# Attention and experts on one core: the spread of the softmax sums moved from GpSimd to VectorE's reciprocal, with four smaller moves around the first pairs

## The chip, the cores and the metric

The kernel runs on one core of a Trainium2 chip. The core's engines are PE (TensorE, matmuls and transposes), DVE (VectorE), ACT (ScalarE) and POOL (GpSimd); SP only issues transfers. Each runs its own instructions in the order in which they stand, and waits for the others through semaphores. The metric is device time of one execution in microseconds, as the median of several runs.

## The reference, cut to what matters

```python
q, k, v: (2, 8, 1152, 64)           # batch, heads, positions, head size
q_pool = q.reshape(B, H, S // 2, 2, D).mean(axis=3)      # 576 pooled rows a head
scores = scale * q_pool @ k.T
scores = scores - scores.max(-1)
attn = exp(scores)
attn = attn / (attn.sum(-1) + 1e-09)
x = attn @ v                         # then to (B * S / 2, H * D) = (1152, 512)
p = domain_probs / (domain_probs.sum(-1) + 1e-09)
for e in range(4):
    out += p[:, e:e + 1] * (relu(x @ w1[e]) @ w2[e])     # 512 -> 1024 -> 512
```

## The kernel before

**Pairs and tiles.** Attention goes over 8 pairs of heads (pair 0 to 7, `n` in the code). A pair has nine tiles of 128 pooled rows by 1152 keys; tiles 0 to 7 belong to one head each, tile 8 holds the last 64 rows of both. Matmuls take fp32 operands split into a high and a low part, so each q and k is split (`pool_split`: POOL writes the high part, then the difference), and k and q halves are moved to the other partitions by transfers within SBUF (`stack_k`, `move_q`).

**The way of a tile.** PE writes its scores to PSUM. DVE reads them once, scales, negates, takes the minimum and writes them to SBUF (`neg_scores`, line 440: called the pass over the scores below). ACT takes exp and sums each row (`exps`). PE transposes the result in blocks of 64, ACT and DVE copy half of the transposed blocks each (`transposed`, lines 336 and 338), and PE multiplies by v (`PV_part`, line 472).

**Rounds.** A pair has five rounds (`round_`, `r` from 0 to 4), each for two tiles, round 3 for one. In a round PE transposes a finished tile, writes scores of a tile three ahead, transposes the seam (the last block of one tile and the first of the next), writes the second scores, transposes the second tile, and does a part of the product with v. PSUM has two sides for scores, which are used in turn, so that new scores wait until DVE's pass has read the old ones of that side.

**Blocks prepared for later pairs.** At the end of a round PE transposes blocks for other purposes into a side of PSUM that is free by then (`prepare`): the next pair's q (`item_q`) and k (`item_k`), and the inverse sums (`item_r`). With `defer` the copy out of PSUM is put off until the next round has transposed its first tile (`waiting`). In round 3 of pairs 1 to 5 the blocks of the next k stand `beside` the seam in the same PSUM region `tp`.

**The sums.** The output of a group of tiles is scaled by 1 / sum. `inv_sums` runs in round 0 (for the pair before, tiles 4 to 8) and in round 2 (tiles 0 to 3): DVE adds 1e-9 and takes the reciprocal of 4 or 5 numbers a row, POOL copies each of the first four over 64 columns into `spread` (line 481), PE transposes `spread` at the end of the round, and DVE copies the result to `rb`.

**Behind a round.** What an output tile needs afterwards (its split, or sums and differences of blocks for the Strassen-like scheme of the experts) is put in `behind` and runs on POOL, in pair 6 with `all_split`: three sums and four splits in a row. POOL also prepares w1 in the last pairs (`w1_sums`, `w1_lo`).

**The start.** SP issues q and k of pair 0, then of pair 1, then v of pair 0 and the stacking of its k (`stack_k0`), held behind a marked instruction by a `nop` on SP (`behind_q`).

```python
pn, grp, k0, k1 = ((n - 1, 1, 0, 5), (n - 1, 1, 5, 9), (n, 0, 0, 3), (n, 0, 3, 6), (n, 0, 6, 9))[r]
```

That line of `round_` says which pair's and group's product with v, and which of the nine key blocks, stand in which round.

Of the kernel before, what the change touches and what calls it, by code (L numbers as in the profile page):

```python
# [17 lines left out]
def attention_moe_kernel(ctx, tc, q, k, v, probs, w1, w2, out):  # L18
    nc = tc.nc
    B, H, S, D = q.shape  # L20
    NT, DM = out.shape
    E, _, FF = w1.shape
    P = 128
# [124 lines left out]
    with ExitStack() as actx:  # L148
# [122 lines left out]

        def join_k(c, dst=None):
            t0, t1 = KTS[c]
            nc.gpsimd.tensor_copy(
                (kc[c] if dst is None else dst).rearrange("p (t h d) -> p t h d", h=2, d=D), kn[:, :, t0:t1].rearrange("p h t d -> p t h d"))

        def split_k(n, c, src):
# [56 lines left out]
        def copy(eng, dst, src):  # L334
            if eng is nc.scalar:
                nc.scalar.activation(dst, src, AF.Copy)  # L336
            else:
                nc.vector.tensor_copy(dst, src)  # L338

        def prepare(items, pt, defer=False):  # L340
            blocks = [b for bl, _ in items for b in bl]
            pt = half_transposes(blocks, pt)

            def used():
                at = 0
                for bl, use in items:
                    use(pt[:, :, at:at + len(bl)])
                    at += len(bl)
            return used if defer else used()

        tiles = []
        for n in range(NP):
# [93 lines left out]
            nc.scalar.activation(sx[g % 3], sx[g % 3], AF.Exp, bias=mn[g % 3], scale=-1.0,  # L446
                                 accum_out=sums[n % 2][:, i:i + 1])

        def transposed(parts, pt, engs):
            pt = half_transposes([sx[g % 3][:, kt * P:(kt + 1) * P] for g, k0, k1 in parts for kt in range(k0, k1)], pt)  # L450
            at = 0
            for g, k0, k1 in parts:
                n, i = tiles[g]
                src = pt[:, :, at:at + k1 - k0]
                at += k1 - k0
                if i == 8:
                    dst = aT[1][:, :, k0:k1, 256:320]
                else:
                    j, h = divmod(i, 2)
                    dst = aT[j // 2][:, h, k0:k1, (j % 2) * P:(j % 2 + 1) * P].rearrange("p k (a x) -> p a k x", a=2)  # L460
                if len(engs) == 1:
                    copy(engs[0], dst, src)
                else:
                    for a in range(2):
                        copy(engs[a], dst[:, a], src[:, a])

        def PV_part(n, grp, k0, k1):
            po = PVB
# [7 lines left out]
        def inv_sums(n, grp):  # L476
            c0, c1 = ((0, 4), (4, 9))[grp]
            r = rs[n % 2][:, c0:c1]
            nc.vector.tensor_scalar_add(r, sums[n % 2][:, c0:c1], 1e-9)
            nc.vector.reciprocal(r, r)  # L480
            nc.gpsimd.tensor_copy(
                spread.rearrange("p (c x) -> p c x", x=HALF), r[:, :4].unsqueeze(2).to_broadcast([P, 4, HALF]))

        def split_x(op, kt, c, src, eng):
            hi, lo = xop(op, 0, kt)[:, c], xop(op, 1, kt)[:, c]
# [97 lines left out]
        neg_scores(1)  # L583
        join_k(0)
        join_k(1)
        join_k(2, xr[:, 1, :4 * P])
        prep_q0()
        summed = add_q(nc.gpsimd)
        behind_q = nc.sync.nop()
        tc.add_manual_dep(behind_q.ins, summed.ins.name, SYNC, reason="loads behind the second q")  # L590
        load_kv(vn[0], v, 0)
        stack_k0()
        scores(2, 1, 0, True)
# [18 lines left out]
        both = (nc.scalar, nc.vector)  # L612
        pending = [2]
        first = [1]
        waiting = []

        def round_(n, r, items=(), spare=(), beside=(), wide=False, before=None, mid=None, defer=False, swap=True):
            ts_ = [g for g in ((9 * n + 5,) if r == 3 else [9 * n + (-1, 1, 3, 0, 6)[r] + j for j in range(2)]) if g >= 0]
            x, count, side = ts_[0], len(ts_), first[0]
            f = x + 3  # L620
            transposed([(x, 0, 8)], tp, both)
            while waiting:
                waiting.pop(0)()
            if before:
                before()
            rest = scores(f, count, side, wide)
            transposed([(x, 8, 9)] + [(g, 0, 1) for g in ts_[1:]], tp, both[:1])
            if beside:
                prepare(beside, tp[:, :, HALF:])
            for g in pending:  # L630
                exps(g)
            pending.clear()
            neg_scores(f)
            if count == 2:
                scores2(f + 1, rest)
                transposed([(ts_[1], 1, 9)], tp, both)
                exps(f)
                neg_scores(f + 1)
            pending.append(f + count - 1)
            if mid:  # L640
                mid()
            pn, grp, k0, k1 = ((n - 1, 1, 0, 5), (n - 1, 1, 5, 9), (n, 0, 0, 3), (n, 0, 3, 6), (n, 0, 6, 9))[r]
            if pn >= 0:
                PV_part(pn, grp, k0, k1)
                if k1 == KT:
                    finish(pn, grp)
            if items:
                used = prepare(items, SIDE[side if count == 2 else 1 - side], defer)
                if defer:
                    waiting.append(used)  # L650
                if count == 2 and swap:
                    first[0] = 1 - side
            if spare:
                prepare(spare, tp)
            while behind:
                behind.pop(0)()

        for n in range(NP):
# [3 lines left out]
            if n == 0:  # L662
                round_(0, 0, [item_k(1, 1, nc.scalar), item_k(1, 2, nc.scalar)], wide=True)
            elif n == 1:
                round_(1, 0, [item_k(2, 1, nc.scalar), item_k(2, 2, nc.scalar)], [item_r(0, 1, nc.vector)],
                       before=lambda: inv_sums(0, 1), defer=True)
            else:
                round_(n, 0, [item_r(n - 1, 1, nc.vector)], before=lambda: inv_sums(n - 1, 1))
            if n and two:
# [10 lines left out]


            if n == 0:
                round_(0, 1, [item_q(1, nc.scalar)], wide=True, mid=lambda: stack_k(1, 0, 4), swap=False)
            elif n == 1:
                round_(1, 1, [item_q(2, nc.scalar)], defer=True)
                stack_k(2, 0, 4)
            else:
                round_(n, 1)
                if not last:
                    move_q(n + 1, 1)  # L690
# [6 lines left out]
            if n == 1:  # L697
                round_(n, 2, r0, before=lambda: inv_sums(n, 0))
                move_q(2, 0)
                stack_k(2, 4, 9)  # L700
                move_q(2, 1)
            else:
                round_(n, 2, r0, before=lambda: inv_sums(n, 0), swap=n > 0)
            if n == 0:
                stack_k(1, 4, 9)
                move_q(1, 1)
# [17 lines left out]


            if n and two:
                round_(n, 3, [item_q(n + 2, nc.scalar)], beside=[item_k(n + 2, 1, nc.scalar)], defer=True)
            else:
                round_(n, 3)
            if n and not last:  # L730
# [8 lines left out]


            if n and two:
                round_(n, 4, [item_k(n + 2, 2, nc.scalar)], defer=True)
                stack_k(n + 2, 0, 4)
            else:
                round_(n, 4)
# [190 lines left out]
```

## Time and profile before

| what | value |
|---|---|
| median of 3 runs | 640.75 us (639.38 to 641.59) |
| the profiled execution | 640.39 us, span 638.6 us |
| PE busy | 610.0 us, 96% of the span |
| DVE, ACT, POOL busy | 362.5, 297.5, 347.5 us |
| attention with its way out | 0 to about 264 us |
| experts | about 264 to 638.6 us |
| mean granted clock of PE | 0.982 |

The times of rows and windows are counted in the profiled execution from the start of its span. Busy time counts an engine's instructions whether or not the next engine waits for them, so what an engine is worth is read from who waits for whom. [...]

### The profile page before, as it was taken

What the parts mean: (1) busy time and instruction counts of PE and PEld (TensorE: products, weight loads), DVE (VectorE), ACT (ScalarE), POOL (GpSimd) and SP (SyncE); (2) the same over time, 40 slices, a digit from 0 to 9 for tenths busy, and PEclk for the clock granted to TensorE, in tenths of its full rate; (3) what the DMA queues carried; (4) which work ended last, traced back from release to release, by engine and by line L of the source; (5) the groups of instructions that cost most, each with busy time, mean ns of one, the idle gap of its engine ahead of it and who ended that gap; (6) DMA issues with size and microseconds to landing.
All of it is one profiled execution on the core that took longest, in us unless ns stands there. A gap on an engine that the chain in (4) does not pass through costs nothing.

```text
span 638.6 us, 12467 instructions
## 1 busy us (share of the span) xinstructions
PE 610.0 (96%) x5045; PEld 515.2 (81%) x5045; DVE 362.5 (57%) x564; ACT 297.5 (47%) x545; POOL 347.5 (54%) x411
## 2 busy tenths in 40 slices
PE   8888899999999688999999999999999999999997
PEld 7656677777777566799899899899889889989986
DVE  6667486787877563954544454454454454454454
ACT  5756567677776553462343243144144135135030
POOL 4626635446460664795674584584484485485140
PEclk9999799999999977999999999999999999999999
DMA  4793684673925100111111111121121121120105
GB/s 149 166 246 102 150 209 126 129 189 98 217 63 154 34 26 9 59 41 53 48 34 51 49 46 55 34 65 35 35 66 34 34 67 33 34 67 1 33 2 148
DMA packets 41497, 50.90 MB, mean 80 GB/s; under 512 B 3296, under 2 KB 27232, under 8 KB 41440
## 3 DMA queue, kind: packets, MB, share of 16 engines
q1 hardware_dynamic: 40560, 48.94, 29.3%
q10 hardware_dynamic: 880, 1.18, 0.5%
q8 instruction: 39, 0.64, 0.4%
q14 instruction: 18, 0.15, 0.1%
HBM read 30.97 MB, written 2.36 MB: 52 GB/s over the span
## 4 chain that ended last, share of the span: by engine, by line
PE 87%; POOL 5%; DMA 2%; ACT 2%; issue 1%; DVE 1%; SPq 0%; POOLq 0%; DVEq 0%
PE banks L892 31%; PE banks L137 27%; PE banks L472 10%; PE banks L207 8%; PE banks L388 8%; PE banks L380 3%; DMA kk<-kk 2%; POOL xb L490 1%; DVE sx L440 1%; POOL q2all L215 1%; POOL xb L487 1%; ACT aT L336 1%; DMA kq<-in_k_dram 0%; POOL kk L118 0%; ACT sx L446 0%
## 5 line engine op out<-in xcount | busy, mean ns | idle before, releaser
L892 PE MATMUL banks<-w2s,hb 128*128 128x512 f32 (+1 forms) x876 | 199.3, 387 | 0.0
L892 PEld LDWEIGHTS banks<-w2s,hb 128*128 128x128 f32 x876 | 162.5, 188 | 32.7
L896 DVE SCALAR_TENSOR_TENSOR acc<-banks,pw,acc 128x512 f32<-128x512 f32 (+1 forms) x137 | 101.7, 743 | 81.4 <-PE banks L892 81.2
L118 POOL TENSOR_TENSOR kk<-kq,kk 128x512 fp32r<-128x512 f32 x64 | 72.6, 1169 | 116.4 <-ACT kk L110 116.4
L440 DVE TENSOR_SCALAR_CACHE_REDUCE sx<-banks 128x1152 f32<-128x1152 f32 x72 | 97.3, 1352 | 32.3 <-PE banks L207 30.6
L336 ACT ACTIVATE aT<-banks 128x512 f32<-128x512 f32 (+1 forms) x144 | 59.6, 437 | 77.8 <-PE banks L207 76.3
L446 ACT ACTIVATE sx<-sx,mn 128x1152 f32<-128x1152 f32 x72 | 90.7, 1259 | 0.5 <-DVE sx L440 0.5
L812 POOL TENSOR_TENSOR hb<-xr,hb 128x576 fp32r<-128x576 f32 x48 | 68.9, 1444 | 21.0 <-ACT hb L811 21.0
L472 PE MATMUL banks<-aT,vn 128*64 128x320 f32 (+1 forms) x576 | 80.2, 419 | 0.0
L859 ACT ACTIVATE xr<-banks 128x576 f32<-128x576 f32 x14 | 9.1, 653 | 147.7 <-PE banks L137 147.7
L137 PE MATMUL banks<-xb,kk 128*128 128x288 f32 x480 | 76.9, 296 | 0.4 <-ACT xr L819 0.4
L137 PE MATMUL banks<-q2all,kk 128*128 128x288 f32 x448 | 75.1, 296 | 0.0
L388 PE MATMUL banks<-kk,q2all 64*128 64x512 f32 (+1 forms) x504 | 67.9, 385 | 3.2 <-DMA kk<-kk 2.4
L137 PEld LDWEIGHTS banks<-xb,kk 128*128 128x128 f32 x480 | 68.3, 189 | 1.1 <-ACT xr L819 0.6
L207 PEld LDWEIGHTS banks<-ident,sx 64*128 64x128 f32 x1296 | 56.1, 143 | 15.2 <-ACT aT L336 6.9
L207 PE MATMUL banks<-ident,sx 64*128 64x64 f32 x1296 | 66.6, 231 | 1.3 <-DVE rb L338 0.7
L338 DVE COPY aT<-banks 128x512 f32<-128x512 f32 x72 | 49.6, 689 | 26.8 <-PE banks L207 25.8
L137 PEld LDWEIGHTS banks<-q2all,kk 128*128 128x128 f32 x448 | 64.5, 188 | 0.0
L808 DVE TENSOR_TENSOR xr<-banks,xr 128x576 f32<-128x576 f32 x48 | 36.4, 758 | 40.0 <-PE banks L137 39.8
L472 PEld LDWEIGHTS banks<-aT,vn 128*64 128x64 f32 x576 | 38.3, 139 | 24.5 <-issue 1.2
L388 PEld LDWEIGHTS banks<-kk,q2all 64*128 64x128 f32 x504 | 52.3, 195 | 6.5 <-issue 3.1
L137 PE MATMUL banks<-xa,kk 128*128 128x288 f32 x384 | 56.7, 296 | 0.0
(105 smaller groups left out, 627.6 us busy)
## 6 DMA issues: line engine op xcount, KB each, us to landing
kq<-in_moe_w_dram SPq DMA_DIRECT2D x64, 128.0 KB, 2.4
qsf<-in_moe_w_dram SPq DMA_DIRECT2D x16, 512.0 KB, 3.5
q2all<-q2all SPq DMA_DIRECT2D x28, 256.0 KB, 7.5
vn<-in_v_dram SPq DMA_DIRECT2D x8, 576.0 KB, 5.1
kk<-kk SPq DMA_DIRECT2D x14, 320.0 KB, 8.6
kq<-in_k_dram SPq DMA_DIRECT2D x7, 576.0 KB, 6.2
kq<-in_q_dram SPq DMA_DIRECT2D x7, 576.0 KB, 4.1
kk<-kk SPq DMA_DIRECT2D x14, 256.0 KB, 3.8
```

The source lines that it names most:

```text
L118: nc.gpsimd.tensor_tensor(flat(w1s[u % 2][:, 1, a:b]), flat(wf[:, a:b]), flat(w1s[u % 2][:, 0, a:b].bitcast(F32)), ALU.subtract)
L137: nc.tensor.matmul(chain[:, c, :CW], w1s[u % 2][:, a, WI[wo], kt, :], xop(xo, z, kt)[:, c * CW:(c + 1) * CW], start=(first and kt == 0 and ...
L207: nc.tensor.transpose(pt[:, a, j, :], src[r], ident[r, r])
L336: nc.scalar.activation(dst, src, AF.Copy)
L338: nc.vector.tensor_copy(dst, src)
L388: return nc.tensor.matmul(dst, q2[n % 2][ROWS[a], zq, h, t * P:(t + 1) * P], src[n % 2][ROWS[a], zk, cs], start=(j == 0), stop=(j == 2), s ...
L440: nc.vector.tensor_scalar(sx[g % 3].rearrange("p (c x) -> p c x", c=c), view, -INV, None, ALU.mult, ALU.min, accum_out=mn[g % 3])
L446: nc.scalar.activation(sx[g % 3], sx[g % 3], AF.Exp, bias=mn[g % 3], scale=-1.0, accum_out=sums[n % 2][:, i:i + 1])
L472: nc.tensor.matmul(po[h * HALF:(h + 1) * HALF, :w], vn[n % 2][:, h, kt, :], aT[grp][:, h, kt, :], start=(kt == 0), stop=(kt == KT - 1))
L812: nc.gpsimd.tensor_tensor(lo, c, hi.bitcast(F32), ALU.subtract)
L892: nc.tensor.matmul(pc, h[:, a, sl, ts_], w[:, b, sl, c0:c1], start=(m == 0), stop=(m == len(ops) - 1))
L896: nc.vector.scalar_tensor_tensor(ac, pc, pw[:, tt, e:e + 1], ac, ALU.mult, ALU.add)
```

## The change

`inv_sums` writes DVE's reciprocal straight to `spread`, 64 columns for each of the four numbers; a second reciprocal makes the ninth tile's inverse in place. POOL's copy is gone. `defer` and `waiting` are gone: prepared blocks are copied out of PSUM as soon as they are transposed. `beside` blocks are transposed in one go with the seam, and both are read after. In pair 0 the sum of the second q moves from POOL to DVE, its copy from ACT to DVE and ahead of the second pass over the scores (`ahead`), and in round 2 of pair 0 both halves of the first tile's copy go to ACT (`heads`). SP's `nop` waits for the join of the second k instead of the sum of q. In pair 1 the inverse sums are transposed ahead of the next k's blocks.

```diff
         def join_k(c, dst=None):
...
-            nc.gpsimd.tensor_copy(
+            return nc.gpsimd.tensor_copy(
...
-        def prepare(items, pt, defer=False):
-            blocks = [b for bl, _ in items for b in bl]
-            pt = half_transposes(blocks, pt)
-
-            def used():
-                at = 0
-                for bl, use in items:
-                    use(pt[:, :, at:at + len(bl)])
-                    at += len(bl)
-            return used if defer else used()
+        def blocks_of(items):
+            return [b for bl, _ in items for b in bl]
+
+        def use_items(items, pt, at=0):
+            for bl, use in items:
+                use(pt[:, :, at:at + len(bl)])
+                at += len(bl)
+
+        def prepare(items, pt):
+            use_items(items, half_transposes(blocks_of(items), pt))
...
-        def transposed(parts, pt, engs):
-            pt = half_transposes([sx[g % 3][:, kt * P:(kt + 1) * P] for g, k0, k1 in parts for kt in range(k0, k1)], pt)
+        def transposed(parts, pt, engs, beside=()):
+            blocks = [sx[g % 3][:, kt * P:(kt + 1) * P] for g, k0, k1 in parts for kt in range(k0, k1)]
+            pt = half_transposes(blocks + blocks_of(beside), pt)
...
+            use_items(beside, pt, at)
...
             nc.vector.tensor_scalar_add(r, sums[n % 2][:, c0:c1], 1e-9)
-            nc.vector.reciprocal(r, r)
-            nc.gpsimd.tensor_copy(
+            nc.vector.reciprocal(
                 spread.rearrange("p (c x) -> p c x", x=HALF), r[:, :4].unsqueeze(2).to_broadcast([P, 4, HALF]))
+            if grp:
+                nc.vector.reciprocal(r[:, 4:], r[:, 4:])
...
-        join_k(2, xr[:, 1, :4 * P])
+        joined = join_k(2, xr[:, 1, :4 * P])
+        behind_k = nc.sync.nop()
+        tc.add_manual_dep(behind_k.ins, joined.ins.name, SYNC, reason="loads behind the second k")
         prep_q0()
-        summed = add_q(nc.gpsimd)
-        behind_q = nc.sync.nop()
-        tc.add_manual_dep(behind_q.ins, summed.ins.name, SYNC, reason="loads behind the second q")
         load_kv(vn[0], v, 0)
         stack_k0()
...
-            transposed([(x, 0, 8)], tp, both)
-            while waiting:
-                waiting.pop(0)()
+            transposed([(x, 0, 8)], tp, heads)
...
-            transposed([(x, 8, 9)] + [(g, 0, 1) for g in ts_[1:]], tp, both[:1])
-            if beside:
-                prepare(beside, tp[:, :, HALF:])
+            transposed([(x, 8, 9)] + [(g, 0, 1) for g in ts_[1:]], tp, both[:1], beside)
...
+            def prepared():
+                if spare:
+                    prepare(spare, tp)
+                if items:
+                    prepare(items, SIDE[side if count == 2 else 1 - side])
...
                 exps(f)
+                if ahead:
+                    prepared()
                 neg_scores(f + 1)
...
-            if items:
-                used = prepare(items, SIDE[side if count == 2 else 1 - side], defer)
-                if defer:
-                    waiting.append(used)
-                if count == 2 and swap:
-                    first[0] = 1 - side
-            if spare:
-                prepare(spare, tp)
+            if not ahead:
+                prepared()
+            if items and count == 2 and swap:
+                first[0] = 1 - side
...
-                round_(0, 1, [item_q(1, nc.scalar)], wide=True, mid=lambda: stack_k(1, 0, 4), swap=False)
+                round_(0, 1, [item_q(1, nc.vector)], wide=True, before=lambda: add_q(nc.vector), mid=lambda: stack_k(1, 0, 4),
+                       ahead=True, swap=False)
...
-                round_(n, 2, r0, before=lambda: inv_sums(n, 0), swap=n > 0)
+                round_(n, 2, r0, before=lambda: inv_sums(n, 0), heads=both if n else both[:1] * 2, swap=n > 0)
...
-                round_(n, 3, [item_q(n + 2, nc.scalar)], beside=[item_k(n + 2, 1, nc.scalar)], defer=True)
+                round_(n, 3, [item_q(n + 2, nc.scalar)], beside=[item_k(n + 2, 1, nc.scalar)])
```

The other calls of `round_` with `defer=True` lose that argument. Three places show how the instructions stand.

On DVE, in round 2 of a pair (`rs` are the sums of four tiles, `sx` the pass over the scores, `aT` the copy of half a transposed tile, `rb` the spread inverse), it stood before:

```order
L338 COPY aT_89<-banks 128x8x64
L479 TENSOR_SCALAR rs_100<-sums_98 128x4
L480 RECIPROCAL rs_100<-rs_100 128x4
L440 TENSOR_SCALAR sx_86,mn_95<-banks 128x1152
L338 COPY aT_90<-banks 128x8x64
L440 TENSOR_SCALAR sx_87,mn_96<-banks 128x1152
L338 COPY rb_91<-banks 128x2x2x64
```

and with the change:

```order
L338 COPY aT_89<-banks 128x8x64
L481 TENSOR_SCALAR rs_100<-sums_98 128x4
L482 RECIPROCAL spread<-rs_100 128x256
L440 TENSOR_SCALAR sx_86,mn_95<-banks 128x1152
L338 COPY aT_90<-banks 128x8x64
L440 TENSOR_SCALAR sx_87,mn_96<-banks 128x1152
L338 COPY rb_91<-banks 128x2x2x64
```

The order is the same; the reciprocal writes 256 columns instead of 4.

On POOL, where pair 6 passes into pair 7 (`xb` and `q2all` are operands of the experts that are split there, `kq` holds w1), it stood before:

```order
L487 TENSOR_SCALAR xb<-xr 128x256
L490 TENSOR_TENSOR xb<-xr,xb 128x256
L97 TENSOR_TENSOR kq<-kq 128x256 x4
L481 COPY spread<-rs_100 128x256
L487 TENSOR_SCALAR q2all<-xr 128x576
L490 TENSOR_TENSOR q2all<-xr,q2all 128x576
L118 TENSOR_TENSOR kk_74<-kq,kk_74 128x512
```

and with the change:

```order
L490 TENSOR_SCALAR xb<-xr 128x256
L493 TENSOR_TENSOR xb<-xr,xb 128x256
L97 TENSOR_TENSOR kq<-kq 128x256 x4
L490 TENSOR_SCALAR q2all<-xr 128x576
L493 TENSOR_TENSOR q2all<-xr,q2all 128x576
L118 TENSOR_TENSOR kk_74<-kq,kk_74 128x512
```

The copy that stood behind the splits and the sums of w1 is gone there, as in fifteen other places.

On SP, in pair 0 (`vn` is v, `kk_74` the stacking of the first k, `kk_75` that of the second, `q2all` the q of pair 1), the difference is:

```order
 L174 DMA vn_84<-in_v_dram 128x2x576
 L265 DMA kk_74<-kk_74 64x1152 x4
+L293 DMA q2all<-q2all 64x4x256 x2
 L285 DMA kk_75<-kk_75 64x2x512 x2
-L293 DMA q2all<-q2all 64x4x256 x2
 L285 DMA kk_75<-kk_75 64x2x640 x2
```

The move of the second q now stands ahead of the first part of the second k; v and the first stacking stay in front of both, behind another instruction of POOL.

## Rows read from the trace of the kernel before

**Rows 1.** The waits of PE in total; columns: us, times, longest us
```profile
PE banks L207 <- POOL spread L481: 11.7, 3, 5.6
```

**Rows 2.** Timeline of PE, pair 7: start us, us, what, [idle before <-releaser]
```profile
223.52 0.48 PE L207 MATMUL banks<-ident,spread 64*128 64x64 f32 x4 [5.03 <-POOL spread L481]
...
242.28 0.47 PE L207 MATMUL banks<-ident,spread 64*128 64x64 f32 x4 [5.56 <-POOL spread L481]
```

**Rows 3.** Windows: us, busy PE, PEld, DVE, ACT, POOL; PEclk, DMA share, GB/s
```profile
223.52:231.94 8.42, 8.42 (x76) 6.57 (x77) 4.80 (x9) 4.63 (x9) 3.23 (x3) 0.62 0.01 2
137.77:143.59 5.82, 5.82 (x79) 4.23 (x78) 4.75 (x9) 4.00 (x8) 0.00 (x0) 1.00 1.08 223
242.28:248.58 6.30, 6.30 (x43) 4.74 (x44) 2.33 (x3) 1.91 (x3) 4.67 (x6) 0.63 0.07 21
203.26:207.57 4.31, 4.31 (x45) 3.15 (x43) 2.87 (x5) 2.72 (x5) 0.00 (x0) 1.00 0.53 167
66.72:74.90 8.18, 8.18 (x87) 6.14 (x87) 1.88 (x2) 4.28 (x8) 4.05 (x5) 0.62 0.58 147
124.23:129.93 5.70, 5.65 (x86) 4.49 (x86) 3.10 (x5) 4.51 (x8) 3.77 (x5) 1.00 0.15 34
36.68:42.00 5.32, 5.32 (x72) 4.29 (x73) 3.76 (x7) 3.74 (x8) 0.05 (x1) 1.00 1.07 289
126.50:129.93 3.43, 3.38 (x60) 2.96 (x56) 2.06 (x3) 2.80 (x7) 2.22 (x3) 1.00 0.23 51
143.59:146.84 3.25, 3.25 (x57) 2.89 (x55) 2.93 (x5) 1.74 (x4) 2.10 (x4) 1.00 0.91 172
```

**Rows 4.** Groups of DVE by shape: count, busy us, mean ns, idle before
```profile
L480 DVE RECIPROCAL rs<-rs 128x4 f32<-128x4 f32 x8 | 1.4, 178 | 0.3
...
L480 DVE RECIPROCAL rs<-rs 128x5 f32<-128x5 f32 x8 | 1.5, 191 | 0.3
...
L606 DVE RECIPROCAL prs<-prs 128x18 f32<-128x18 f32 x1 | 0.3, 268 | 0.0
...
L338 DVE COPY rb<-banks 128x256 f32<-128x256 f32 x16 | 6.8, 422 | 19.6 <-PE banks L207 19.6
```

**Rows 5.** Timeline of DVE, round 2 of pair 4 and of pair 6
```profile
145.76 0.18 DVE L480 RECIPROCAL rs<-rs 128x4 f32<-128x4 f32 x1
145.85 1.33 DVE L440 TENSOR_SCALAR_CACHE_REDUCE sx<-banks 128x1152 f32<-128x1152 f32 x1
...
147.71 1.35 DVE L440 TENSOR_SCALAR_CACHE_REDUCE sx<-banks 128x1152 f32<-128x1152 f32 x1
...
200.63 1.36 DVE L440 TENSOR_SCALAR_CACHE_REDUCE sx<-banks 128x1152 f32<-128x1152 f32 x1 [0.26 <-PE banks L207]
```

**Rows 6.** Timeline of PE, rounds 0 and 3 of pair 4
```profile
134.92 2.91 PE L472 MATMUL banks<-aT,vn 128*64 128x320 f32 x20
...
149.12 1.94 PE L380 MATMUL banks<-kk,q2all 128*128 128x512 f32 x9
...
151.75 0.46 PE L207 MATMUL banks<-ident,qsf 64*128 64x64 f32 x8 [0.49 <-ACT aT L336]
```

**Rows 7.** Timelines of POOL, SP's queue and PE, pairs 0 and 1
```profile
13.48 0.62 POOL L274 COPY xr<-kq 128x512 f32<-128x512 f32 x1
...
18.79 0.38 SPq L174 DMA_DIRECT2D vn<-in_v_dram  x1
...
36.68 1.27 PE L388 MATMUL banks<-kk,q2all 64*128 64x512 f32 x10 [2.42 <-DMA kk<-kk]
```

**Rows 8.** Timelines of DVE and PE behind the last pair
```profile
262.33 0.49 DVE L499 TENSOR_TENSOR xr<-banks,rb 128x320 f32<-128x320 f32 x1
...
264.23 1.07 PE L137 MATMUL banks<-xb,kk 128*128 128x288 f32 x6 [0.37 <-ACT xr L819]
```

**Rows 9.** Timeline of PE, pair 1
```profile
61.37 0.34 PE L207 MATMUL banks<-ident,spread 64*128 64x64 f32 x4 [1.12 <-POOL spread L481]
...
66.72 0.69 PE L207 MATMUL banks<-ident,qsf 64*128 64x64 f32 x8 [2.44 <-POOL qsf L274]
```

More of the change, by code (lines that the diff above doesn't have):

```diff
@@ L614, in attention_moe_kernel, with round_ @@
         first = [1]
-        waiting = []
-        def round_(n, r, items=(), spare=(), beside=(), wide=False, before=None, mid=None, defer=False, swap=True):
+        def round_(n, r, items=(), spare=(), beside=(), wide=False, before=None, mid=None, ahead=False, heads=both, swap=True):
             ts_ = [g for g in ((9 * n + 5,) if r == 3 else [9 * n + (-1, 1, 3, 0, 6)[r] + j for j in range(2)]) if g >= 0]
@@ L665, in attention_moe_kernel @@
                 round_(1, 0, [item_k(2, 1, nc.scalar), item_k(2, 2, nc.scalar)], [item_r(0, 1, nc.vector)],
-                       before=lambda: inv_sums(0, 1), defer=True)
+                       before=lambda: inv_sums(0, 1))
             else:
@@ L682, in attention_moe_kernel @@
             if n == 0:
-                round_(0, 1, [item_q(1, nc.scalar)], wide=True, mid=lambda: stack_k(1, 0, 4), swap=False)
+                round_(0, 1, [item_q(1, nc.vector)], wide=True, before=lambda: add_q(nc.vector), mid=lambda: stack_k(1, 0, 4),
+                       ahead=True, swap=False)
             elif n == 1:
-                round_(1, 1, [item_q(2, nc.scalar)], defer=True)
+                round_(1, 1, [item_q(2, nc.scalar)])
                 stack_k(2, 0, 4)
@@ L741, in attention_moe_kernel @@
             if n and two:
-                round_(n, 4, [item_k(n + 2, 2, nc.scalar)], defer=True)
+                round_(n, 4, [item_k(n + 2, 2, nc.scalar)])
                 stack_k(n + 2, 0, 4)
```

## The prediction, made before the changed kernel was run

> **What bounds the kernel now.** I read the waits of PE first, since PE does 96% of the span, then the PE timeline at each long wait, then the windows around it for the granted clock, and last the timelines of the engines that PE waits for. PE waits 11.7 us in three places for line 481, POOL's spread copy [rows 1]. Two of them lie in the last pair and take 5.03 and 5.56 us [rows 2]: the copy itself is short, but it is queued on POOL behind the differences and splits of pair 6, and PE has to have it before round 0 and round 2 of pair 7 can end. The third, 1.12 us, is in pair 1 [rows 9].
>
> Behind such a wait PE goes on at a lower clock. [...] So the two waits cost 2.60 and 1.99 us more than they show. From 264.2 on PE streams the experts' products [rows 3, 8]; nothing there is touched.
>
> Between these ends, in pairs 2 to 5, PE hardly waits, but DVE is close behind it. In round 2 of pair 4 DVE's second pass over the scores (line 440) runs from 147.71 to 149.06, and PE's next scores, which overwrite those banks, start at 149.12 [rows 5, 6]. The slack of DVE against PE at that place is 0.06 us. That is the number to remember, since the change puts work on DVE just ahead of it.
>
> **What the change costs and gives.** The sums are made against the profiled execution, 640.39 us (span 638.6); the median of the three runs is 640.75, so 0.36 is added at the end.
>
> *The reciprocal.* It wrote 4 or 5 elements a row and now writes 256. No row shows 256. Its rows are 178 ns for 4 elements, 191 for 5 and 268 for 18 [rows 4]: from 4 to 18 each element costs 90/14 = 6.4 ns. Carried on, 256 elements take 0.268 + 238 x 0.0064 = 1.80 us, which is 1.62 more than now. Below, the nearest row with 256 elements is the copy of line 338 at 0.42 us [rows 4]. Above, the step from 4 to 5 is 13 ns, and 0.268 + 238 x 0.013 = 3.36 us. I take 1.80: it is the slope over 14 elements, the 13 ns one over a single element, and the 0.42 is another operation. [...]
>
> *Round 2 of each pair.* Behind the reciprocal on DVE's queue stand the pass over the scores that PE has finished, the copy of half a transposed tile, and the second pass. PE waits for each of these: the spread's transposes need the first pass to have read their banks, the next tile's transposes need the copy, the next scores the second pass. All three start 1.62 later, so PE's scores of 149.12 start 1.62 - 0.06 = 1.56 later, in pairs 2 to 5: 4 x 1.56 = 6.2. In pairs 6 and 7 DVE waits 0.26 for PE ahead of the first pass [rows 5], which absorbs that much: 2 x 1.30 = 2.6. DVE doesn't carry the delay on, because it waits for PE in the round after.
>
> *Round 0.* The same reciprocal and one for the ninth tile stand there, but PE covers them with 20 products of line 472 (2.91 us [rows 6]) where round 2 has 12. I take 0.1 for each of six pairs, 0.6; the low end is 0, and every further 0.1 us of the instruction would show in full.
>
> *Pair 1.* The 1.12 us for the spread go [rows 9], but DVE's second pass is late by about as much as PE gains; and the gate weights' sums behind it on DVE are waited for by POOL, which joins the k that PE wants at 66.72. I take a loss of 0.6, half of that wait; a gain of 1.7 if the reciprocal is short. The 2.44 us wait at 66.72 stays, and its slow clock too.
>
> *Behind pair 7* DVE is the chain: it ends with line 499 at 262.33, and PE's stream starts at 264.23 [rows 8]. Ahead of it stands the last spread reciprocal with the small one: 1.62 + 0.18 = 1.8.
>
> *The spread copies on POOL.* Removing them removes the two waits of rows 2, 10.6 us, and the low clock behind them, 4.6. What is next there is POOL's own work for pair 7's operands and w1; it no longer stands in front of PE, and it runs through without the gaps in which it waited for PE. At worst it takes back the clock's 4.6.
>
> *v and the first stacking.* SP sent v at 18.79, held until POOL had added q [rows 7]. Now it waits only for the third join, which ends at 14.10 [rows 7]: up to 4.7 us earlier. These five transfers (1.7 MB by their shapes) stood in front of those that PE waits for at 36.68, for 2.42 us [rows 7]. SP's queue now has the q move ahead of the second k's first half; it still waits for a POOL split, so the last stack can't leave 4.7 earlier. I take the wait itself, 2.4; the low end is 0. The add of q goes to DVE where DVE waited for PE, so it is hidden; without that cover its 640 columns would cost 640/256 x 0.42 = 1.05 us, an estimate by the copy of [rows 4].
>
> *Copies at once, the blocks beside the seam.* In round 3 PE waited 0.49 us for ACT to read the seam before it transposed the next k's blocks [rows 6]; now both are transposed in one go and ACT reads after. Four pairs (2 to 5): 2.0. In round 4 ACT's copy of q held PE's second scores: from the tile's transposes to the products with v that round took 3.43 us, round 2 3.25 [rows 3]. That is 0.18 in four pairs, 0.7. ACT's other copies then start a little later, into time in which it waited for PE.
>
> *Sum.* Gains 10.6 + 4.6 + 2.4 + 2.0 + 0.7 = 20.3; losses 6.2 + 2.6 + 0.6 + 0.6 + 1.8 = 11.8; net 8.5 faster. 640.39 - 8.5 = 631.9, on the median's scale 632.3 us.
>
> **Rivals.** *A, the reciprocal is cheap:* at 0.42 us the extra is 0.24, round 2 loses 4 x 0.18 = 0.7, the end 0.4, pair 1 gains 1.7. Gains 22.0, losses 1.1: 619.9. For it speaks only that other operations of DVE run at that rate; against it the 268 ns for 18 elements.
>
> *B, the reciprocal is dearer, and DVE becomes the bound:* beyond 1.80 us every added microsecond counts in rounds 0 and 2 of six pairs, in pair 1 and at the end, about 14 times. It decides from 1.80 + 8.5/14 = 2.4 us, 9.0 ns an element; there nothing is gained, and beyond it the kernel is slower. At the 13 ns step it is 3.36 us, and 632.3 + 14 x 1.56 = 654.1. For it: the 13 ns step from 4 to 5. Against it: the 77 ns from 5 to 18, 5.9 each. [...]
>
> *C, the new waits in round 2 lower the clock* as the wait of 2.44 us at 66.72 did: the stretch behind it took 8.18 us at 0.62, its like in pair 3 took 5.70 at 1.00 [rows 3], 2.48 more. In six pairs that is 14.9, and 647.2. It decides if four pairs are hit (9.9). Against it: after the wait of 2.42 us at 36.68 the clock stayed at 1.00 [rows 3], and the new waits are 1.56 in all, in three pieces with work between.
>
> *D, the first stacking brings nothing,* because the transfers are late by the q move: 634.7, within the likeliest one's range.
>
> **How the numbers follow.** The likeliest case with D: 0.58, its own range 628 to 636. A dearer reciprocal that still gains (7.5 to 9 ns, 635 to 640): 0.16. A: 0.13. B beyond 9 ns: 0.07. C: 0.06. The range 620.5 to 639.5 leaves out B, C and about half of A. No change, for three or five rounds of this kernel, is about 0.3%, here 638.8 to 642.7. Faster by more: 0.58, A's 0.13 and most of the 0.16, 0.83. Slower: B beyond 642.7 and C, 0.11. Within: 0.06.
>
> **What would show it.** The reciprocal's group: 16 of 128x256 with a mean near 1.8 us. PE's waits without POOL's spread, with waits for DVE instead, about 1.6 us in round 2 of each pair, and the distance from one pair to the next up from 27.5 (124.23 to 151.75 [rows 3, 6]) to about 28.4. PE's clock at 9 tenths between 215 and 250. PE's first rows of pair 1 at about 34.3. No wait for ACT ahead of the k blocks in round 3. I am wrong if the reciprocal's mean lies under 1 or over 2.4 us, if the clock drops inside the pairs, or if POOL holds PE in the last pair at another instruction.

## The result, and the profile after

| | before | after |
|---|---|---|
| median | 641.17 us (4 runs, 639.38 to 642.38) | 634.59 us (4 runs, 633.87 to 635.43) |
| ratio | 1 | 0.990, 95% interval 0.9873 to 0.9928 |
| profiled execution; span | 640.39; 638.6 us | 635.43; 633.6 us |
| mean granted clock of PE, a share of full speed | 0.982 | 0.991 |

The change makes the kernel 6.6 us faster by the medians, 5.0 by the two profiled spans; 8.5 was forecast. What follows is read from the profiled executions, so it adds up to 5.0. In the changed kernel the spread reciprocal is line 482, the product with v 474, the output tile's scaling 502, SP's relay 398.

PE's waits in total, the longest groups (us, times, longest us):

```profile
PE banks L380 <- DVE sx L440: 3.9, 7, 0.6
PE banks L207 <- ACT aT L336: 2.9, 6, 0.6
PE banks L207 <- POOL qsf L274: 2.7, 1, 2.7
PE banks L388 <- SPq L398: 2.3, 1, 2.3
PE banks L474 <- DVE xr L502: 1.8, 1, 1.8
PE banks L207 <- DVE sx L440: 1.7, 4, 0.4
PE banks L207 <- DVE aT L338: 1.3, 7, 0.2
```

POOL's spread [rows 1] is gone from the list. New are many short waits for DVE, one of 1.8 us for DVE behind pair 7, and one of 2.3 us for SP. The reciprocal's groups on DVE (count, busy us, mean ns):

```profile
L482 DVE RECIPROCAL spread<-rs 128x256 f32<-128x256 f32 x16 | 28.0, 1753 | 0.6
...
L485 DVE RECIPROCAL rs<-rs 128x1 f32<-128x1 f32 x8 | 0.8, 104 | 0.0
```

PE's timeline in pair 7, where [rows 2] stood, and behind it:

```profile
236.70 0.34 PE L207 MATMUL banks<-ident,spread 64*128 64x64 f32 x4 [0.45 <-DVE sx L440]
...
251.12 3.45 PE L474 MATMUL banks<-aT,vn 128*64 128x320 f32 x24 [1.80 <-DVE xr L502]
```

Windows there (us, busy time of PE, PEld, DVE, ACT, POOL, then PEclk, DMA share, GB/s):

```profile
225.48:231.40 5.92, 5.92 (x78) 4.35 (x76) 5.37 (x11) 4.76 (x12) 5.67 (x9) 1.00 0.00 0
...
236.70:243.00 6.30, 5.53 (x61) 4.11 (x62) 4.17 (x8) 4.32 (x9) 6.05 (x9) 1.00 0.00 0
```

No wait of 5 us is left, and the clock is 1.00 where it was 0.62 and 0.63 [rows 3].

Where the time went is read from the starts of equal instructions in the two traces. In the kernel before:

```profile
40.85 0.71 PE L207 MATMUL banks<-ident,sx 64*128 64x64 f32 x16
...
204.04 1.95 PE L380 MATMUL banks<-kk,q2all 128*128 128x512 f32 x9
...
265.14 1.75 PE L137 MATMUL banks<-q2all,kk 128*128 128x288 f32 x12
```

In the changed kernel:

```profile
67.42 0.69 PE L207 MATMUL banks<-ident,qsf 64*128 64x64 f32 x8 [2.66 <-POOL qsf L274]
...
211.11 1.94 PE L380 MATMUL banks<-kk,q2all 128*128 128x512 f32 x9 [0.56 <-DVE sx L440]
...
260.13 1.75 PE L137 MATMUL banks<-q2all,kk 128*128 128x288 f32 x12
```

The transposes at 66.72 of [rows 9] start at 67.42: **0.70 lost** in the start and pair 1 (forecast: 1.8 gained). Split at the transposes of 40.85, which now start at 42.29 (shown below under the start), that is 1.44 lost in the start, where 2.4 gained were forecast, and 0.74 gained in pair 1, where 0.6 lost were forecast. From there to the end of pair 6 another **6.4 are lost**: the scores of round 3 of pair 6 move from 204.04 to 211.11, which is 7.07 in all (forecast: 5.3 for that stretch, 6.2 + 2.6/2 + 0.5 of round 0 less 2.0 and 0.7). Pair 7 and what follows **gain 12.1**: the experts' products that stood at 265.14 start at 260.13, 5.01 earlier (forecast: 12.0 for that stretch, 10.6 + 4.6 less 1.3, 0.1 and 1.8). So the misses lie at the start and inside the pairs. That the end is right to 0.1 is in part luck. Round 2 of pair 7 costs 1.6 and not 1.3: from the products with v at 234.74 to the scores at 238.58 it is 3.84 us, and in pair 6 of the kernel before it was 2.23. Against that the wait of 0.37 for ACT of [rows 8], for which the forecast had no term, is gone.

**Round 2 of pair 4**, on DVE and then on PE:

```profile
148.57 0.74 DVE L481 TENSOR_SCALAR rs<-sums 128x4 f32<-128x4 f32 x1
149.34 1.75 DVE L482 RECIPROCAL spread<-rs 128x256 f32<-128x256 f32 x1
```

```profile
150.42 1.52 PE L474 MATMUL banks<-aT,vn 128*64 128x256 f32 x12
...
152.37 0.34 PE L207 MATMUL banks<-ident,spread 64*128 64x64 f32 x4 [0.43 <-DVE sx L440]
...
152.97 0.71 PE L207 MATMUL banks<-ident,sx 64*128 64x64 f32 x15 [0.20 <-DVE aT L338]
154.24 1.94 PE L380 MATMUL banks<-kk,q2all 128*128 128x512 f32 x9 [0.56 <-DVE sx L440]
```

The delay reaches PE in three waits of 0.43, 0.20 and 0.56, which add up to 1.19; the rest shows as no wait, only in the starts. From the products with v to these scores it is 3.82 us (150.42 to 154.24), where it was 2.28 (146.84 to 149.12, [rows 3, 6]): 1.54 more, 1.56 was forecast.

**Round 4 of pair 3**, on ACT and on PE:

```profile
130.57 0.81 ACT L336 ACTIVATE raw<-banks 128x768 f32<-128x768 f32 x1 [0.86 <-POOL kk L215]
131.27 0.59 ACT L336 ACTIVATE aT<-banks 128x512 f32<-128x512 f32 x1
```

```profile
131.92 0.34 PE L207 MATMUL banks<-ident,sx 64*128 64x64 f32 x4 [0.59 <-ACT aT L336]
```

This was not forecast. ACT's copy of q, now made at once, writes `raw`, from which POOL still splits the next k; it waits 0.86 us for that, and ACT's half of the transposed tile, which PE needs, stands behind it. From the tile's transposes at 129.46 to the products with v at 133.45 it is 3.99 us, where [rows 3] had 3.43.

**The start**, on PE and on SP's queue:

```profile
37.51 0.32 PE L388 MATMUL banks<-kk,q2all 64*128 64x128 f32 x1 [2.33 <-SPq L398]
...
39.53 2.83 PE L474 MATMUL banks<-aT,vn 128*64 128x256 f32 x12
42.29 0.82 PE L207 MATMUL banks<-ident,sx 64*128 64x64 f32 x16
```

```profile
33.15 1.26 SPq L170 DMA_DIRECT2D kq<-in_q_dram  x1
34.45 0.95 SPq L174 DMA_DIRECT2D kq<-in_k_dram  x1
35.45 0.47 SPq L174 DMA_DIRECT2D vn<-in_v_dram  x1
35.96 1.44 SPq L601 DMA_DIRECT2D pr<-in_moe_domain_probs_dram  x2
```

PE no longer waits for the stacked k. It waits, almost as long, for a `nop` on SP: the relay of `S_rows`. This `nop` waits for one matmul of PE, and a later matmul waits for the `nop`; the reason given in the code is "row tiles of one bank". The relay stands on SP's queue behind four loads and can't run until the last is issued at 37.40. Behind this wait the granted clock is 0.67 on average from 37.51 to 42.29, and 12 products with v take 2.83 us, where they took 1.52 before; before, the 2.42 us wait of [rows 7] lay over the relay, and the clock stayed at 1.00 [rows 3].

### The profile page after: what moved, and what is told of

Its sections match the earlier page's. It is cut to its first block, busy times and chain, and to the rows that moved or that the text cites. A ratio compares the mean times of both kernels' runs of the same rounds, so it can differ in the third digit from the quotient of the medians.

```text
span 633.6 us, 12423 instructions
## 1 busy us (share of the span) xinstructions
PE 608.9 (96%) x5045; PEld 512.6 (81%) x5045; DVE 386.9 (61%) x575; ACT 296.9 (47%) x545; POOL 339.1 (54%) x392
## 4 chain that ended last, share of the span: by engine, by line
PE 84%; DVE 9%; ACT 2%; POOL 2%; issue 2%; SPq 1%; DMA 1%; POOLq 0%; DVEq 0%
PE banks L895 31%; PE banks L137 28%; PE banks L474 9%; PE banks L207 7%; PE banks L388 6%; DVE sx L440 4%; PE banks L380 3%; DVE spread L482 2%; DVE aT L338 2%; POOL kk L215 1%; ACT aT L336 1%; DVE rs L481 1%; ACT raw L336 1%; DMA kq<-in_k_dram 1%; POOL kk L214 0%
## 5 line engine op out<-in xcount | busy, mean ns | idle before, releaser
L336 ACT ACTIVATE aT<-banks 128x128 f32<-128x128 f32 (+1 forms) x145 | 60.0, 437 | 60.3 <-PE banks L207 60.0
L207 PE MATMUL banks<-ident,sx 64*128 64x64 f32 x1296 | 68.6, 229 | 4.5 <-ACT aT L336 2.9
L388 PE MATMUL banks<-kk,q2all 64*128 64x512 f32 (+1 forms) x504 | 66.4, 376 | 2.3 <-SPq L398 2.3
```

The source lines that it names most:

```text
L207: nc.tensor.transpose(pt[:, a, j, :], src[r], ident[r, r])
L388: return nc.tensor.matmul(dst, q2[n % 2][ROWS[a], zq, h, t * P:(t + 1) * P], src[n % 2][ROWS[a], zk, cs], start=(j == 0), stop=(j == 2), s ...
```

## The experiments

My theory after the result: the gain is the two waits of pair 7 with their low clock; the losses are the reciprocal's 1.75 us in round 2, the copy of q made at once in round 4, and the relay on SP, which takes the place of the transfer. The rival: the moves around the reciprocal carry the gain, and the spread by itself gives back what it takes.

**One part alone: the spread.** The kernel before with the new `inv_sums`.

```diff
-            nc.vector.reciprocal(r, r)
-            nc.gpsimd.tensor_copy(
+            nc.vector.reciprocal(
                 spread.rearrange("p (c x) -> p c x", x=HALF), r[:, :4].unsqueeze(2).to_broadcast([P, 4, HALF]))
+            if grp:
+                nc.vector.reciprocal(r[:, 4:], r[:, 4:])
```

> The kernel before with one part of the change alone: the spread by DVE's reciprocal, everything else as it was. My theory: this part carries the gain. It ends the two waits of PE for POOL's spread in the last pair and the low clock behind them (12.1 us in the stretch from pair 7 on, as the changed kernel's trace showed), gives back some 0.7 in pair 1, and costs 1.54 in round 2 of pairs 2 to 5 and 1.05 in pair 6 (7.2): net -5.6, so about 635.6 us against 641.2 of before, and round 4 of pairs 2 to 5 stays at 3.43 us from the tile's transposes to the products with v. Rival: the moves around it (first stacking, copies at once, beside the seam) carry the gain and the long reciprocal takes back what it gives: 639 to 642.

Measured: 637.25 us, ratio 0.9945 (0.9923 to 0.9966), so 3.5 us faster (2.2 to 4.9); the profiled span is 633.0, 5.6 shorter. PE's scores of round 3, in pairs 3, 4 and 5:

```profile
124.86 1.94 PE L380 MATMUL banks<-kk,q2all 128*128 128x512 f32 x9 [0.56 <-DVE sx L440]
...
153.93 1.94 PE L380 MATMUL banks<-kk,q2all 128*128 128x512 f32 x9 [0.56 <-DVE sx L440]
...
182.44 1.94 PE L380 MATMUL banks<-kk,q2all 128*128 128x512 f32 x9 [0.56 <-DVE sx L440]
```

Scores of round 3 start at 95.81, 124.86 and 153.93 in pairs 2 to 4, 29.06 apart, where it was 27.52: the reciprocal costs 1.54 a pair there, and 28.51 - 27.46 = 1.05 in pair 5. By the medians the part alone makes somewhat more than half of the 6.6 us; the time lies between the 635.6 of my theory and the rival's 639 to 642. Its 11 runs lie between 635.0 and 641.3, with the clock between 0.985 and 0.993. In the profiled one (635.15) 12 products with v take 1.77 us at 29.95, with no wait ahead of them, and 1.52 at 34.59. Why time is lost there, and clock in the others, isn't shown.

**The other parts alone.** The changed kernel with DVE's small reciprocal and POOL's copy (the diff above, reversed).

> The changed kernel with the spread as it was before: a small reciprocal on DVE and POOL's copy over 64 columns. My theory: the waits of about 5 us in pair 7 come back with their low clock (+12.1), pair 1 loses 0.7, round 2 of pairs 2 to 6 gets back 7.2: about 634.6 + 5.6 = 640.2 us, no faster than before. Rival: the other moves carry the gain: 634 to 636.

Measured: 639.55 us, ratio 0.9974 (0.9958 to 0.9989), 1.7 faster than before. PE's waits:

```profile
PE banks L207 <- POOL spread L483: 12.4, 3, 5.5
```

The two waits are back (5.04 and 5.55), and all the moves together are worth 1.7 us. So the spread carries the gain: next to these moves it is worth 5.0 us (639.55 to 634.59). Its pairs are 27.37 us apart, so the moves gain 0.15 a pair, not the 0.49 + 0.18 that I had put down.

**The reciprocal made short.** DVE takes the small reciprocal and copies it over 64 columns itself.

```diff
-            nc.vector.reciprocal(
+            nc.vector.reciprocal(r, r)
+            nc.vector.tensor_copy(
                 spread.rearrange("p (c x) -> p c x", x=HALF), r[:, :4].unsqueeze(2).to_broadcast([P, 4, HALF]))
-            if grp:
-                nc.vector.reciprocal(r[:, 4:], r[:, 4:])
```

> The changed kernel, but DVE takes the reciprocal of the 4 or 5 numbers and then copies them over 64 columns itself: 0.18 or 0.19 us and about 0.42 instead of 1.75. My theory: in round 2 the delay of DVE shows nearly in full, so 1.15 us come back in round 2 of pairs 2 to 7 and in the chain behind pair 7, some 0.5 more in pair 1: 7 x 1.15 + 0.5 = 8.5, about 626 us. Rival 1: the second pass over the scores is late for another reason, and the length of the reciprocal is hidden: 634 to 635. Rival 2: only the part over DVE's slack counts and the copy of a broadcast column is as slow as the reciprocal (1.7 us): no change, 634.6, and the copy's rows show it.

Measured: 629.53 us, ratio 0.9833 (0.9807 to 0.9858), 5.1 us below the changed kernel by the medians and 4.3 by the ratios, where 8.5 was expected. The copy takes longer than expected. DVE, in round 2 of pair 4 and of pair 5:

```profile
146.12 0.75 DVE L481 TENSOR_SCALAR rs<-sums 128x4 f32<-128x4 f32 x1
146.90 0.18 DVE L482 RECIPROCAL rs<-rs 128x4 f32<-128x4 f32 x1
147.12 1.12 DVE L483 COPY spread<-rs 128x256 f32<-128x256 f32 x1
...
175.11 0.42 DVE L483 COPY spread<-rs 128x256 f32<-128x256 f32 x1
```

POOL in round 2 of pair 4:

```profile
145.97 0.88 POOL L215 TENSOR_TENSOR xa<-xr,xa 128x320 fp32r<-128x320 f32 x1
146.79 1.30 POOL L185 TENSOR_TENSOR qsf<-kq 128x512 f32<-128x512 f32 x1
```

The same copy takes between 0.29 and 1.26 us (mean 0.87 over 16). In pair 4 it ends at 148.24, 0.15 behind POOL's sum of q, which ends at 148.09. The addition of four numbers ends at 146.87, with POOL's instruction that ends at 146.85. So two of DVE's three instructions seem to wait for POOL, not ahead of their start, as for a semaphore, but within their own duration; the next run tests it. The pairs from 2 to 4 are 28.55 apart, the next two 27.31.

**The same without POOL's influence.** The copy is written as a sum over one element. By my theory it takes 0.3 to 0.45 us in all 16 places, whether POOL runs or not, and the time is about 626 us.

```diff
-            nc.vector.tensor_copy(
-                spread.rearrange("p (c x) -> p c x", x=HALF), r[:, :4].unsqueeze(2).to_broadcast([P, 4, HALF]))
+            nc.vector.tensor_reduce(
+                spread.rearrange("p (c x) -> p c x", x=HALF),
+                r[:, :4].unsqueeze(2).to_broadcast([P, 4, HALF]).unsqueeze(3), AX.X, ALU.add)
```

> [...] As a copy it took 0.29 us where POOL was idle and 1.12 to 1.26 us where POOL ran, 0.87 on average, and ended when POOL's instruction ended. [...] Rival: reading one number 64 times is what is slow (then the sum takes 0.9 us on average too), or DVE's second pass is late for another reason: 629.5.

Measured: 626.07 us, ratio 0.9762 (0.9741 to 0.9782). The group on DVE, and its round 2 of pair 4:

```profile
L483 DVE TENSOR_REDUCE spread<-rs 128x256 f32<-128x256 f32 x16 | 6.7, 420 | 0.5
```

```profile
143.84 0.74 DVE L481 TENSOR_SCALAR rs<-sums 128x4 f32<-128x4 f32 x1
...
144.83 0.42 DVE L483 TENSOR_REDUCE spread<-rs 128x256 f32<-128x256 f32 x1
```

Every one takes 0.42 us, this one too, while POOL runs the same sum of q (144.52, 1.29 us). The rival, that reading a number 64 times is slow, falls. The addition ahead of it still takes 0.74. The pairs are 27.83 apart, where 27.7 was expected.

**The addition left out as well.** The kernel leaves out the 1e-9 that the reference adds to the sums.

```diff
-            nc.vector.tensor_scalar_add(r, sums[n % 2][:, c0:c1], 1e-9)
-            nc.vector.reciprocal(r, r)
+            nc.vector.reciprocal(r, sums[n % 2][:, c0:c1])
```

> As the run with the sum over one element, and the addition of 1e-9 is left out (a sum of exponentials relative to the largest is at least 1, and 1e-9 is lost beside it in fp32). That addition of 4 numbers took 0.20 us where POOL was idle and 0.75 where it ran. My theory: DVE's share in round 2 then falls under the slack, the pairs are 27.4 us apart as they are with POOL's spread, and the time is 0.3 us per pair below the run with the addition: 624 to 625 us. Rival: the pairs are bound by PE already without this, and nothing is gained: as the run with the addition.

Measured: 623.74 us, ratio 0.9721 (0.9704 to 0.9738). PE's scores of round 3 in pair 4:

```profile
146.52 1.94 PE L380 MATMUL banks<-kk,q2all 128*128 128x512 f32 x9
```

They start without a wait, 27.31 behind those of pair 3 (119.21). In pairs 2 to 5 round 2 is PE's again; in pair 6 PE still waits 0.30 there for DVE's second pass.

**The copy of q put off again.** As before the change, for `item_q` in round 3 alone.

```diff
+        def prepare_late(items, pt):
+            pt = half_transposes(blocks_of(items), pt)
+            waiting.append(lambda: use_items(items, pt))
...
             transposed([(x, 0, 8)], tp, heads)
+            while waiting:
+                waiting.pop(0)()
...
-                    prepare(items, SIDE[side if count == 2 else 1 - side])
+                    (prepare_late if late else prepare)(items, SIDE[side if count == 2 else 1 - side])
```

> The changed kernel, but ACT's copy of q out of PSUM in round 3 of pairs 1 to 5 is put off again until round 4 has transposed its first tile. My theory: copied at once it stands ahead of ACT's half of that tile's copy, and waits for POOL, which still reads the buffer for the k's split; PE waits 0.59 us behind it. Put off, round 4 goes from 3.99 back to 3.43 us in pairs 2 to 5: -2.2, about 632.4 us, and PE's wait for ACT's aT in round 4 is gone. Rival: ACT is late there because of the exp ahead of it, and putting the copy off brings nothing: 634.6.

Measured: 632.86 us, ratio 0.9878 (0.9854 to 0.9903). PE's transposes beside the seam in pairs 3 and 4:

```profile
125.21 0.41 PE L207 MATMUL banks<-ident,qsf 64*128 64x64 f32 x8
```

```profile
153.80 0.41 PE L207 MATMUL banks<-ident,qsf 64*128 64x64 f32 x8
```

28.59 apart, against 28.98 in the changed kernel (127.25 to 156.23): 0.4 a pair, where 0.56 was expected; PE's waits for `aT` fall from 2.9 us in 6 places to 0.5 in 2. The span is 3.1 shorter; by the medians it is 1.4 to 1.7, of the intervals' size. Against the spread alone (29.06 apart) these pairs gain 0.47: that is the seam, forecast at 0.49, with round 4's copy of k still made at once.

**The relay set free.** The second v and the probabilities are loaded behind round 4 of pair 0.

```diff
                 load_kv(kn, k, 2)
-                load_kv(vn[1], v, 1)
-                load_probs()
...
                 round_(n, 4)
+            if n == 0:
+                load_kv(vn[1], v, 1)
+                load_probs()
```

> The changed kernel, but the loads of the second v and of the gate's probabilities go out behind round 4 of pair 0 instead of ahead of round 3. In the changed kernel PE waits 2.33 us at 37.51 for a relay on SP's queue that stands behind those loads (SP issues them until 37.40). My theory: SP is free from 35.45 on, PE waits about 0.3 instead of 2.33, the clock does not drop behind it (12 products with v 2.83 us, 1.52 at full clock): 2.0 + 1.3 at the start, of which pair 1 may swallow up to all in its wait for POOL at 67.42 (that wait follows DVE, which follows PE, so I expect most to stay): 631.5 to 633. Rival 1: pair 1's wait swallows it: 634.6 with an earlier PE at 42 and the same at 67.42. Rival 2: PE waits for something else at 37.5, such as the stacked k: no change there at all.

Measured: 631.40 us, ratio 0.9849 (0.9825 to 0.9873), 3.2 below the changed kernel. PE:

```profile
35.93 0.32 PE L388 MATMUL banks<-kk,q2all 64*128 64x128 f32 x1 [0.34 <-SPq L398]
...
37.81 1.52 PE L474 MATMUL banks<-aT,vn 128*64 128x256 f32 x12
39.26 0.71 PE L207 MATMUL banks<-ident,sx 64*128 64x64 f32 x16
```

The wait is 0.34 instead of 2.33, the products take 1.52 instead of 2.83, and the transposes at 42.29 start at 39.26. Pair 1 doesn't swallow it: 67.42 becomes 64.56. Both rivals fall.

**The earlier stacking undone.** `behind_q` and POOL's sum of q come back.

```diff
-        joined = join_k(2, xr[:, 1, :4 * P])
-        behind_k = nc.sync.nop()
-        tc.add_manual_dep(behind_k.ins, joined.ins.name, SYNC, reason="loads behind the second k")
+        join_k(2, xr[:, 1, :4 * P])
         prep_q0()
+        summed = add_q(nc.gpsimd)
+        behind_q = nc.sync.nop()
+        tc.add_manual_dep(behind_q.ins, summed.ins.name, SYNC, reason="loads behind the second q")
```

> The changed kernel, but v and the first k's stacking are held until the second q is summed on POOL, as before the change (the q sum goes back from DVE to POOL for that). My theory: sending them earlier brought nothing, since PE waits for the relay on SP's queue in place of the transfer: within 1 us of 634.6, and if anything faster, since before the change the clock stayed at 1.00 behind that wait (633.5 to 634.6). Rival: the earlier stacking does bring the 2.4 us that I forecast, and another part of the start lost them: about 637.

Measured: 635.46 us, ratio 0.9912 (0.9893 to 0.9931), 0.9 above the changed kernel, within the intervals. I was right on the size and wrong on the sign: PE waits longer for the transfer,

```profile
37.17 2.29 PE L388 MATMUL banks<-kk,q2all 64*128 64x512 f32 x11 [3.47 <-DMA kk<-kk]
```

and is at 43.82 where the changed kernel is at 42.29, of which 0.4 is left at the end of the span. The earlier stacking does its work; the relay hides it.

**The gate weights behind the joins**, in pair 1.

```diff
-            if n == 1:
-                gate_weights()
             if n and two:
                 add_q(nc.gpsimd)
                 join_k(0)
                 join_k(1)
+            if n == 1:
+                gate_weights()
```

> The changed kernel, but in pair 1 POOL's products for the gate weights stand behind the sum of q and the joins of the next k instead of ahead of them. In the changed kernel PE waits 2.66 us at 67.42 for the last of those joins, at which the gate weights, which wait for DVE's sums until 63.63, hold POOL for 2.5 us. My theory: the joins then start when their transfer and the split ahead of them allow, PE's wait goes, and with it the low clock behind it (products with v 2.83 us instead of 1.52, the stretch 67.42 to 76 at 0.66): -2.7 to -5, so 630 to 632 us. Rival: the joins wait for the transfer of q and k or for the pieces of kq, and it stays at 634.6.

Measured: 632.21 us, ratio 0.9868 (0.9844 to 0.9891). The wait of 2.66 us at 67.42 (2.44 before, [rows 9]) is gone:

```profile
64.47 0.46 PE L207 MATMUL banks<-ident,qsf 64*128 64x64 f32 x8
64.87 1.52 PE L474 MATMUL banks<-aT,vn 128*64 128x256 f32 x12
```

The products behind it took 2.83 us in the changed kernel. The span is 3.5 shorter, the median 2.4.

**Together.** First with the copy and the addition still in place:

> The changed kernel with four edits at once: DVE's small reciprocal and its own copy over 64 columns; q's copy in round 3 put off until round 4 has transposed its tile; the second v and the probabilities loaded behind round 4 of pair 0; in pair 1 the gate weights behind the joins. My theory: the gains add, 8.5 + 2.2 + 2 + 3 = 15.7, about 619 us. Rival: each hides behind the next (the round 2 and round 4 waits shift to DVE's passes or POOL's splits): 624 to 628.

Measured: 622.26 us, ratio 0.9711 (0.9686 to 0.9735): 12.3 below the changed kernel, where 15.7 was expected. The four parts alone were 5.1, 1.7, 3.2 and 2.4 us below it, 12.4 in all, so they add up; what is missing was missing in the copy alone, which takes 0.82 us on average here too (0.29 to 1.25). Then with the sum over one element and without the addition:

> All that gained, together: the small reciprocal without the addition, the sum over one element as the spread, q's copy put off into round 4, the second v and the probabilities behind round 4 of pair 0, the gate weights behind the joins. The same with the addition and the copy took 622.3 us. My theory: round 2 gives back what the copy and the addition still cost there (1.2 in pairs 2 to 4, 0.8 in pair 1, 0.9 in the last two places): about 617.5 us. Rival: the next wait (ACT's copies, POOL's splits) takes its place: 620 to 622.

Measured: **616.38 us**, ratio 0.9609 (0.9594 to 0.9624), mean granted clock 1.000. PE's longest groups of waits:

```profile
PE banks L207 <- ACT aT L336: 1.5, 3, 1.0
PE banks L207 <- POOL qsf L274: 1.4, 1, 1.4
```

This version beats both kernels: 18.2 us below the changed one.

## Why the prediction was right, and where it was not

*The reciprocal* was put at 1.80 us and took 1.753 in all 16 places, so rivals A and B fall by their first condition. The 7.5 to 9 ns an element that stand with the chances were an estimate of mine that no run shows; from 18 to 256 elements it was 6.2 ns.

*Round 2* was put at 1.56 in pairs 2 to 5 and 1.30 in pairs 6 and 7. The spread alone shows 1.54 in pairs 2 to 4, and about 1.05 in pairs 5 and 6. The mechanism was right; the term for pair 5 was mis-sized, because I read the slack of 0.06 in pair 4 and carried it to pair 5. There, in the kernel before, DVE already waited for PE ahead of its first pass:

```profile
173.17 1.36 DVE L440 TENSOR_SCALAR_CACHE_REDUCE sx<-banks 128x1152 f32<-128x1152 f32 x1 [0.26 <-PE banks L207]
```

The addition ahead of the reciprocal takes 0.20 us there instead of 0.74, which leaves DVE 0.5 more. In pair 7 it is the other way: the addition, 0.21 us before, takes 0.77 in the changed kernel, and the round costs 1.6 where 1.30 was put. *Round 0* cost nothing where 0.1 a pair was put: in pair 3 the 20 products start 8.66 us ahead of round 1 before and with the spread alone.

*Behind pair 7* the 1.8 stood in the trace as one wait of 1.80. *The spread copies on POOL*: both waits and the low clock went (its 4.6 us are 8.42 - 5.82 and 6.30 - 4.31 in [rows 3]), and POOL holds PE nowhere else there; the stretch gave 12.1 where 12.0 was forecast.

*Rival C* fell too: from 76 to 240 us the clock stays at 1.00, with waits of at most 0.6 us.

*v and the first stacking* is the step that failed: "I take the wait itself, 2.4". The wait went, and a wait of 2.33 for the relay took its place, with a granted clock of 0.67 behind it; the start lost 1.44. The sign that I had named did come, pair 1's first rows at about 34.3 (nine run at 33.74), and said nothing about the gain, since the next row waited. I had looked at the queue in front of the transfer that PE waited for, and not at what else on that queue PE needs next. Rival D had the right result, that nothing is gained, for another reason than the one given there. With the relay free 3.2 us come back. *Pair 1*, put at a loss of 0.6, gained 0.74 and covered a part of this. The spread alone lost 0.14 there; the rest comes from moves for which the forecast had no term in pair 1, and that is luck.

*Copies at once* had the wrong sign: 0.7 gained was forecast, 0.18 in each of four pairs. I had counted that ACT's copy no longer stands ahead of the second scores, and not that it now needs its buffer while POOL reads it. Putting the copy off gives 0.4 a pair back. It is also why the pairs are 28.97 us apart and not 28.4. *The blocks beside the seam* gave 0.47 of 0.49.

So of the forecast 20.3 us of gains, the two terms of pair 7 and the seam held, and the other two, 2.4 and 0.7, turned into losses of 1.44 and about 1.6. That the total still came near has two reasons: round 2 and round 0 lost about 1 us less than forecast, and pair 1 gained by luck.

## What to carry to other kernels

Before a transfer is sent earlier, read what else waits behind it on the same queue, a relay or a `nop` among it: the wait moves to the next thing that PE needs from that queue, and here the granted clock was 0.67 behind the new wait, where it was 1.00 behind the old one. A copy that is made sooner must have its destination free (ACT's copy of q waited 0.86 us for POOL); look for who still reads it. Where DVE is close behind PE, a small instruction is not short because it is small (the addition of 128x4 took from 0.20 to 0.77 us in pairs 1 to 7 of the changed kernel): look at its duration next to POOL's, place by place, and not at its mean.

## What the runs showed of the hardware that was not expected

DVE's copy of 128x256 and its addition of 128x4, both from SBUF to SBUF, took 0.29 and 0.16 us at the least, and 1.24 and 0.78 where an instruction of POOL was under way at their start (at 134.82 in the run with the copy and at 23.62 in the changed kernel). In the kernel before and in the run with the copy, the long additions end within 0.04 us of the end of an instruction of POOL, and the long copies about 0.15 behind one. The 0.20 in pairs 5 and 6, which I had taken for POOL idle, is such a place too: POOL's instruction ends there just under 0.2 us after the addition starts. The reciprocal (1.75 us in 16 places) and the sum over one element (0.42 in 16 places) took the same everywhere. The runs show only which instructions grow beside POOL's, the copy and the addition, and which do not; the reason is not shown. The 0.75 us of that addition in the kernel before, at 144.98, ends 0.03 behind POOL's instruction too; it stood behind the slack of 0.06 us.

From 4 elements on the reciprocal's cost is straight in its elements: 178 ns for 4, 268 for 18, 1753 for 256, which is 90 / 14 = 6.4 and (1753 - 268) / 238 = 6.2 ns for each (one element alone takes 104), against (420 - 219) / 184 = 1.1 for a `tensor_reduce` that reads 256 and 72 elements.
